# Eight strided transfers in place of one for the first weight load of a decode kernel

## The chip, the cores and the metric

The kernel runs on one core of a Trainium2 chip. The metric is the device time of one execution in microseconds; a version's time is the median of its runs.

## The reference

One decode step, with 8 sequences (B), one token each, model width D = 576. Two branches read the same token and a gate mixes them.

```python
x = A_x                                             # [8, 1, 576]
g = sigmoid((x * gate_w).sum(-1, keepdims=True))
# A: attention over a cache, 32 heads of 128, 4096 cached positions
q = (x @ wq).reshape(8, 1, 32, 128).transpose(0, 2, 1, 3)
scores = einsum("bhqd,bhkd->bhqk", q, k_cache) * 128 ** -0.5
o = einsum("bhqk,bhkd->bhqd", softmax(scores), v_cache)
a = o.transpose(0, 2, 1, 3).reshape(8, 1, 4096) @ wo
# B: layer norm, 576 -> 4608, gelu, 4608 -> 576
h = gelu(layernorm(x) @ w1 + b1)
b = h @ w2 + b2
return g * a + (1 - g) * b
```

All tensors are bfloat16. The two caches hold 8 x 32 x 4096 x 128 elements each, 537 MB together; wq and wo are 4.7 MB each, w1 and w2 5.3 MB each.

## The kernel before

**Tiles.** The caches are read in 32 groups (NG), one for 8 heads (HB) of one sequence. A group's K is one tile of 128 partitions x 256 positions x 128 elements, 64 KB for each partition, and its V likewise. K goes to the buffer `KR`, V to the buffer `VB`. Each group is: product of K with the broadcast q on DVE (L499), sums of it on PE (L510 and L189), a last sum on DVE (L522), softmax, then V times the weights on PE (L563).

**Queues.** Big loads are all issued by SP, in the order in which they are written in the program; `load` (L295) issues one transfer with a semaphore of its own, `load_k` (L327) and `load_v` (L338) those of a later group. SP holds back an issue until the buffer that it fills has been read. ACT's queue carries four small loads at the start: x, the gate row, b1, b2. The order at the start of SP's queue is wq (into `VB`, which V does not need yet), two halves of the first K tile, w1 (into the upper part of `KR`), then w2, which waits for the q projection as it overwrites wq's place, then the second K tile, which waits until the first has been multiplied, then the first V.

**wq.** wq is read flat: its 576 x 4096 elements are cut into 128 runs of `WQR` = 18432 elements (36 KB), one for each partition, so a partition holds four and a half rows of wq. That is one transfer with 128 contiguous runs. The list `ld_wq` holds what has to be waited for.

**The q projection.** x is transposed into nine pieces with a mask for odd and even partitions (`transposed`, L424 to L430), and the layer norm's y after it in the same way. Then 36 matmuls of 128x512 (L183 and L189) multiply the pieces of x with wq as it lies. The first of them waits for `ld_wq`. Its result is scaled (L452), spread over the partitions (L464, L468), and one group's q is copied to `q_n` (L474), which the first product with K needs. The issue of w2, and of the first part of V, waits for the last of these matmuls (`p_Q`).

**After the loop.** The last V comes in four parts and wo in five, so that work can begin on each as it lands; two halves of the result go out on SP and ACT.

Of the kernel before, what the change touches and what calls it, by code (L numbers as in the profile page):

```python
# [41 lines left out]
class Stream:  # L42
# [11 lines left out]
    def op(self, engine, fn, waits=(), dma=None, side=0):  # L54

        rec = [fn, [w for w in waits if w is not None], None, dma, (engine, side)]
        self.ops[engine].append(rec)
        if dma is not None:
            return ("dma", *dma)
        return ("op", engine, rec)  # L60
# [84 lines left out]
def bass_gated_mix__mha_block_cached__mixer_channel_mlp__decode_kernel(  # L145
# [18 lines left out]
    op = S.op  # L164
# [7 lines left out]
    def view(t, offset, shape):  # L172
        ap = []
        stride = 1
        for n in reversed(shape[1:]):
            ap.insert(0, [stride, n])
            stride *= n
        return bass.AP(tensor=t, offset=offset, ap=[[pstride(t), shape[0]]] + ap)
# [22 lines left out]
    WQR = D * SK // 128  # L201
    NXH = 2 * D // 128
    wq_sb = view(VB, 0, [128, WQR])
# [90 lines left out]
    def load(engine, dst, src, name, waits=()):  # L294
        return op(engine, lambda e: e.dma_start(dst, src), waits, dma=(nc.alloc_semaphore(name), 16))  # L295
# [6 lines left out]
        return bass.AP(tensor=t.tensor, offset=t.offset, ap=[[0, B], [1, D]])  # L302


    ld_wq = [load("sync", wq_sb, bass.AP(tensor=A_wq.tensor, offset=A_wq.offset, ap=[[WQR, 128], [1, WQR]]), "ld_wq")]


    def kv_src(cache, n):
# [603 lines left out]
```

## Time and profile before

| | |
|---|---|
| median of 3 runs | 1295.15 us (1295.01 to 1296.24) |
| profiled execution | 1295.46 us, span 1293.5 us |
| PE, DVE, ACT busy | 733.1, 854.5, 72.9 us |
| bytes moved by DMA | 557.07 MB, 431 GB/s over the span |
| SP's queue | 99.7% of the time of 16 DMA engines |
| wq, from issue to landing | 13.8 us |

The span runs from the first instruction to the last of the profiled execution; the execution's own time has 2.0 us more around it. A share of DMA is the mean busy share of the core's 16 DMA engines. In short stretches of the span this share and the GB/s are rough, since a transfer's packets are long. The lines of the timeline give an instruction's start and duration in microseconds, engine, line, operation, output and inputs, and in brackets the engine's idle time before it and what ended it. DMA instructions on SPq and ACTq are the issues; the data follow later.

### The profile page before, as it was taken

The page shows a single profiled execution, that of the slowest core. Times are in us where ns is not written, and L with a number is a line of the kernel's source. Part 1 is how long each engine was busy: PE and PEld are TensorE (multiplying, and loading weights), DVE is VectorE, ACT ScalarE, POOL GpSimd, SP SyncE. Part 2 cuts the span into 40 slices and gives each one's busy share as a digit, 9 for nine tenths or more (in the row PEclk, how much of TensorE's full clock was granted, in tenths as well). Part 3 has the DMA queues.
Part 4 walks back from the last instruction along what each step waited for, and adds up shares of the span by engine and source line. Part 5 has one row for each costly group of instructions (what it writes and reads, how often), then busy time and mean ns, then how long its engine had stood idle before and what let it go on. Part 6 is the DMA issues. An engine that isn't in the chain of part 4 may idle for free.

```text
span 1293.5 us, 10984 instructions
## 1 busy us (share of the span) xinstructions
PE 733.1 (57%) x4893; PEld 139.4 (11%) x3047; DVE 854.5 (66%) x1081; ACT 72.9 (6%) x162; POOL 12.3 (1%) x21
## 2 busy tenths in 40 slices
PE   3755556455556555556555556555556555556556
PEld 0211111011111011111011111001111001111003
DVE  4646667766667766667766667766668766667763
ACT  3200000000000000000000000000000000000001
POOL 0100000000000000000000000000000000000001
PEclk8877898787899777888778888877898787799778
DMA  9999999999999999999999999999999999999998
GB/s 405 430 445 424 436 436 428 440 432 428 446 426 434 438 428 436 436 428 444 426 432 442 428 434 438 426 440 432 428 446 426 434 438 428 434 438 428 444 432 344
DMA packets 11440, 557.07 MB, mean 431 GB/s; under 512 B 1416, under 2 KB 1576, under 8 KB 1832
## 3 DMA queue, kind: packets, MB, share of 16 engines
q1 hardware_dynamic: 11232, 556.93, 99.7%
q8 instruction: 5, 0.08, 0.0%
q10 hardware_dynamic: 200, 0.03, 0.0%
q14 instruction: 3, 0.02, 0.0%
HBM read 556.95 MB, written 0.01 MB: 431 GB/s over the span
## 4 chain that ended last, share of the span: by engine, by line
DMA 67%; DVE 18%; PE 9%; issue 5%; DVEq 1%; SPq 0%
DMA KR<-in_A_k_cache_dram 65%; DVE p L499 15%; PE psb L189 8%; DVE s_sb L522 2%; DMA KR<-in_A_wo_dram 2%; PE psb L510 2%; DVEq L522 0%; DVEq L137 0%; SPq L295 0%; PE psb L767 0%; PE psb L464 0%; DVE p L863 0%; DVEq L499 0%
## 5 line engine op out<-in xcount | busy, mean ns | idle before, releaser
L499 DVE TENSOR_TENSOR p<-KR,q_n 128x4096 bf16<-128x4096 bf16 x256 | 581.5, 2282 | 208.3 <-DMA KR<-in_A_k_cache_dram 208.3
L189 PE MATMUL psb<-p,ident 128*128 128x512 bf16 x1792 | 489.0, 419 | 0.0
L510 PE MATMUL psb<-p,ident 128*128 128x512 bf16 x256 | 112.5, 439 | 508.9 <-DVE p L499 508.9
L522 DVE TENSOR_REDUCE s_sb<-psb 128x512 f32 (+1 forms) x256 | 175.1, 684 | 108.6 <-PE psb L189 62.0
L510 PEld LDWEIGHTS psb<-p,ident 128*128 128x128 bf16 x256 | 26.3, 103 | 965.9 <-DVE p L499 965.3
L563 PE MATMUL psb<-VB,P 128*32 128x512 bf16 x1984 | 112.7, 380 | 0.0
L551 DVE TENSOR_SCALAR P<-E,own 128x256 bf16<-128x256 bf16 x256 | 53.5, 282 | 87.4 <-ACT E L548 87.4
L474 ACT ACTIVATE q_n<-q_bc 128x128 bf16<-128x128 bf16 x32 | 9.9, 310 | 873.9 <-DVE p L499 873.8
L563 PEld LDWEIGHTS psb<-VB,P 128*32 128x32 bf16 x1984 | 50.0, 97 | 48.1
L580 PE MATMUL psb<-selO,O_sb 128*128 128x8 f32 x256 | 33.9, 259 | 22.5 <-ACT O_sb L575 22.5
L580 PEld LDWEIGHTS psb<-selO,O_sb 128*128 128x128 f32 x256 | 31.0, 191 | 38.3 <-ACT O_sb L575 38.3
L575 ACT ACTIVATE O_sb<-psb 128x512 f32<-128x512 f32 x32 | 19.1, 597 | 197.5 <-PE psb L563 197.5
L570 PEld LDWEIGHTS psb<-rs,ones 128*128 128x128 f32 x64 | 12.1, 190 | 46.6 <-issue 44.4
L695 POOL TENSOR_TENSOR p<-OT_sb,fine 128x512 bf16<-128x512 bf16 (+1 forms) x4 | 5.0, 1275 | 1199.3 <-PE psb L570 1195.5
L548 ACT ACTIVATE E<-s_sb,mD 128x256 bf16<-128x256 f32 x32 | 16.0, 499 | 0.0
L539 DVE TENSOR_REDUCE mA<-s_sb 128x1 f32<-128x256 f32 x32 | 13.4, 420 | 1.1
L479 ACT ACTIVATE OT_sb<-O_n,G 128x8 bf16<-128x8 f32 x31 | 9.3, 301 | 84.3 <-DVE O_n L586 84.3
L554 DVE TENSOR_REDUCE es<-E 128x1 f32<-128x256 bf16 x32 | 13.1, 410 | 0.0
L570 PE MATMUL psb<-rs,ones 128*128 128x8 f32 x64 | 9.2, 216 | 1.3 <-DVE O_n L586 1.3
L428 PE MATMUL psb<-ident,p 8*128 8x8 bf16 x18 | 0.8, 164 | 15.2 <-ACT p L425 13.5
L555 DVE TENSOR_SCALAR rs<-own,es 128x8 f32<-128x8 f32 x32 | 7.5, 234 | 1.1
L657 PE MATMUL psb<-VB,hT_sb 128*8 128x288 bf16 x72 | 6.4, 354 | 2.6 <-POOL hT_sb L636 2.6
(103 smaller groups left out, 129.6 us busy)
## 6 DMA issues: line engine op xcount, KB each, us to landing
KR<-in_A_k_cache_dram SPq DMA_DIRECT2D x2, 4096.0 KB, 27.8
VB<-in_A_v_cache_dram SPq DMA_DIRECT2D x1, 5376.0 KB, 29.5
KR<-in_B_w_dram SPq DMA_DIRECT2D x1, 5184.0 KB, 45.4
VB<-in_B_w_dram SPq DMA_DIRECT2D x1, 5184.0 KB, 40.3
VB<-in_A_wq_dram SPq DMA_DIRECT2D x1, 4608.0 KB, 13.8
KR<-in_A_v_cache_dram SPq DMA_DIRECT2D x1, 4096.0 KB, 22.3
VB<-in_A_v_cache_dram SPq DMA_DIRECT2D x1, 2816.0 KB, 38.1
KR<-in_A_wo_dram SPq DMA_DIRECT2D x1, 2304.0 KB, 20.7
```

Source lines behind the costliest of these rows:

```text
L189: return e.add_instruction(mybir.InstMatmult(name=nc.get_next_instruction_name(), engine=mybir.EngineType.PE, ins=[e.lower_ap(rhs), e.lowe ...
L499: v_mult[n, c] = op("vector", lambda e: e.tensor_tensor(out=p1[:, par, :, :], in0=k_of(), in1=qb, op=ALU.mult), [k_land[n, s], a_q[n], p_s ...
L510: fn = lambda e, r=r: e.matmul(tr_ps[par][:, :], lhsT=ident[:, :], rhs=r, start=True, stop=False)
L522: v_red[n, c] = op("vector", lambda e: e.tensor_reduce(out=s_of(), in_=tr_ps[par][:, :].rearrange("p (t c) -> p t c", c=CH), axis=AX.X, op ...
L539: t = op("vector", lambda e: e.tensor_reduce(out=mA[:, 0:1], in_=s_sb[:, :], axis=AX.X, op=ALU.max), [v_red[n, NC - 1], c_mA])
L548: a_exp[n] = op("scalar", lambda e: e.activation(out=E[:, :], in_=s_sb[:, :], func=ACT.Exp, bias=mD[:, 0:1], scale=1.0), [v_nm[n], v_P.get ...
L551: v_P[n] = op("vector", lambda e, h=h: e.tensor_scalar(out=P[:, :, h, :], in0=E[:, :].rearrange("p (q t) -> p q t", t=TQ), scalar1=own[:, ...
L554: t = op("vector", lambda e: e.tensor_reduce(out=es[:, :], in_=E[:, :], axis=AX.X, op=ALU.add), [a_exp[n]])
L563: p_pv[n] = op("tensor", lambda e, o=o, tq=tq, at=at, v=v: e.matmul(o, lhsT=P[:, tq, :, :].rearrange("p h t -> p (h t)"), rhs=v.rearrange( ...
L570: p_z[n] = op("tensor", lambda e: e.matmul(oz_ps[:, HB:2 * HB], lhsT=ones[:, :], rhs=rs[:, :], start=True, stop=True), [v_rs[n], v_norm.ge ...
L575: a_ev[n] = op("scalar", lambda e: e.activation(out=O_sb[:].rearrange("p t d -> p (t d)"), in_=o_ps[n // last][:, :], func=ACT.Copy), [p_p ...
L580: p_oz[n] = op("tensor", lambda e, tt=tt: e.matmul(o, lhsT=O_sb[:, tt, :], rhs=selO[:, tt, :], start=(tt == 0), stop=(tt == TQ - 1 and stop)),
```

## The change

wq's load is written as eight transfers instead of one. Transfer i takes the runs i, i + 8, i + 16 and so on, sixteen runs, and writes them to the partitions with the same numbers. So every partition gets the same bytes as before. All eight raise one semaphore, each by 16, and what waits for wq waits for the last count, 128. All eight are issued by SP, one after another, ahead of K.

```diff
-    ld_wq = [load("sync", wq_sb, bass.AP(tensor=A_wq.tensor, offset=A_wq.offset, ap=[[WQR, 128], [1, WQR]]), "ld_wq")]
+    s_wq = nc.alloc_semaphore("ld_wq")
+    for i in range(8):
+        w = bass.AP(tensor=A_wq.tensor, offset=A_wq.offset + i * WQR, ap=[[8 * WQR, 16], [1, WQR]])
+        ld_wq = [op("sync", lambda e, i=i, w=w: e.dma_start(wq_sb[i:128:8, :], w), dma=(s_wq, 16 * (i + 1)))]
```

## The prediction

> **What bounds the kernel now.** I read the page from the top: the shares, the 40 slices, the queues, then the chain that ended last.
>
> ```profile
> span 1293.5 us, 10984 instructions
> ...
> DMA  9999999999999999999999999999999999999998
> GB/s 405 430 445 424 436 436 428 440 432 428 446 426 434 438 428 436 436 428 444 426 432 442 428 434 438 426 440 432 428 446 426 434 438 428 434 438 428 444 432 344
> ...
> q1 hardware_dynamic: 11232, 556.93, 99.7%
> ...
> DMA 67%; DVE 18%; PE 9%; issue 5%; DVEq 1%; SPq 0%
> DMA KR<-in_A_k_cache_dram 65%; DVE p L499 15%; PE psb L189 8%; DVE s_sb L522 2%; DMA KR<-in_A_wo_dram 2%; PE psb L510 2%; DVEq L522 0%; DVEq L137 0%; SPq L295 0%; PE psb L767 0%; PE psb L464 0%; DVE p L863 0%; DVEq L499 0%
> ```
>
> The sixteen DMA engines are busy in every slice, and SP's queue, q1, which carries wq, K, V and the weights, fills 99.7% of their time. Only the first slice (405) and the last (344) fall below the rest. The chain names DVE and PE too, but it walks only the waits of K. To see whether their time is extra I cut the span into stretches: width, busy time (and instructions) of PE, PEld, DVE, ACT, POOL, then the granted clock, the DMA share, GB/s.
>
> ```profile
> 0.00:2.00 2.00, 0.00 (x0) 0.00 (x0) 0.49 (x3) 1.25 (x1) 1.15 (x9) 1.00 0.70 184
> 2.00:4.00 2.00, 0.00 (x0) 0.00 (x0) 1.00 (x3) 1.12 (x3) 0.00 (x0) 1.00 0.54 184
> 4.00:14.50 10.50, 0.38 (x9) 0.32 (x9) 3.99 (x13) 5.47 (x10) 0.30 (x1) 1.00 1.01 431
> 14.50:24.50 10.00, 4.34 (x49) 1.57 (x49) 1.39 (x4) 2.21 (x4) 0.00 (x0) 0.89 1.00 430
> ...
> 100.00:1260.00 1160.00, 657.52 (x4138) 113.45 (x2460) 789.90 (x991) 49.44 (x121) 0.00 (x0) 0.84 1.00 433
> 1260.00:1280.00 20.00, 15.36 (x182) 7.37 (x166) 11.20 (x24) 2.59 (x5) 5.72 (x5) 0.91 0.97 413
> ```
>
> From 4 us on, the engines move 430 to 433 GB/s at a share of 1.00, whatever they read: 433/16 = 27 GB/s for each. That is a cap, and the kernel lives on it. So a microsecond that the DMA engines lose anywhere before 1260 us is lost at the end, unless the queue runs dry somewhere later and has slack to give. It does not: here are SP's issues (start, duration) and the times to landing.
>
> ```profile
> 0.74 0.41 SPq L295 DMA_DIRECT2D VB<-in_A_wq_dram  x1
> 1.21 0.89 SPq L295 DMA_DIRECT2D KR<-in_A_k_cache_dram  x2
> 2.14 0.60 SPq L295 DMA_DIRECT2D KR<-in_B_w_dram  x1
> 19.57 0.33 SPq L295 DMA_DIRECT2D VB<-in_B_w_dram  x1
> 47.77 0.33 SPq L327 DMA_DIRECT2D KR<-in_A_k_cache_dram  x1
> ...
> 91.92 0.33 SPq L327 DMA_DIRECT2D KR<-in_A_k_cache_dram  x1
> 108.78 0.33 SPq L338 DMA_DIRECT2D VB<-in_A_v_cache_dram  x1
> ```
>
> ```profile
> KR<-in_B_w_dram SPq DMA_DIRECT2D x1, 5184.0 KB, 45.4
> VB<-in_B_w_dram SPq DMA_DIRECT2D x1, 5184.0 KB, 40.3
> VB<-in_A_wq_dram SPq DMA_DIRECT2D x1, 4608.0 KB, 13.8
> ```
>
> wq lands at 0.74 + 13.8 = 14.5 us, w1 at 2.14 + 45.4 = 47.5, w2 at 19.57 + 40.3 = 59.9. The second K tile is issued at 47.77, 12.1 us before w2 has drained, so the queue always has its next transfer. From here each K and V follows in the same way.
>
> **The change, part by part.**
>
> *Seven more issues on SP.* The duration of one is in the rows of the helper's line (minimum, median, maximum ns):
>
> ```profile
> L295 SPq DMA_DIRECT2D KR<-in_A_wo_dram x5: 383/433/433, 1225.6 to 1267.1; - x5
> L295 SPq DMA_DIRECT2D KR<-in_A_v_cache_dram x4: 327/374/433, 1253.1 to 1265.2; - x4
> ```
>
> Eight at 0.33 to 0.43 us, 0.05 us between them, take 3.0 to 3.9 us in place of 0.41. The two K halves and w1 stand behind them on SP: K's first issue moves from 1.21 to about 3.8 to 4.6 us, w1's from 2.14 to about 5. K's data are not wanted by the engines before wq has drained near 14.5 us. So this costs 0; were that cover gone, it would cost 2.6 to 3.4 us. w2's issue waits for the q projection, 19.57 us, and does not move for this reason. ACT's queue (x, the gate row, b1, b2) is not passed by anything.
>
> *Feeding the engines.* One new transfer is 576 KB, 0.59 MB; at 433 GB/s it lasts 1.36 us, against an issue of 0.4. The queue stays ahead: 0.
>
> *Joints between transfers.* What seven more joints cost is seen best near the end, where SP issues V's four parts and wo's four:
>
> ```profile
> 1253.12 12.48 SPq L295 DMA_DIRECT2D KR<-in_A_v_cache_dram  x4
> 1265.65 1.85 SPq L295 DMA_DIRECT2D KR<-in_A_wo_dram  x4
> 1291.61 0.37 SPq L868 DMA_DIRECT2D out_dram<-p  x1
> ```
>
> There eight transfers go through in line at 413 instead of 433 GB/s in 20 us: 20 x 20/433 = 0.92 us for eight, 0.8 for seven. The other bound is 0, by wq, K and w1, which join at 431 and 430. I take 0, since wq's runs stay long (36 KB each), like those. [...]
>
> *The first bytes.* The first two stretches move 184 GB/s each: 2 x 2 x (433-184)/433 = 2.3 us are lost, 1.15 us of them by 1.15 us, when the only wq issue ends. If sixteen runs are described sooner than 128, the gain is at most the other 1.15 us. At the other end it is 0. I take -0.2: the engines must in any case fetch their first run, and nothing shows that 0.41 us of issue would shrink.
>
> *The wait.* The q projection waits for one semaphore at 128 instead of one at 16. It is the same wait, on PE, once: 0. Behind it on PE stand only the broadcast of q and the first key sums, which need q.
>
> *Which partitions are written together.* This is the only term with a size. Before, a transfer spans 128 partitions; after, it spans 16 that lie eight apart, and four transfers in a row have offsets 0 to 3 before offsets 4 to 7 come. No row shows a large transfer over a part of the partitions. The cap of 27 GB/s is the same for K, V, wq and the weights, with runs of different lengths, so it is not the source's: it sits either in the sixteen engines or on sixteen paths into the memory that they write. If in the engines, this term is 0. If on the paths, it matters which partitions are hit together: where paths own blocks of four neighbours, every eighth partition reaches every second block alone, two engines stand on one path, and the other half of the paths idle until the fifth transfer. wq's 4.72 MB then take twice 4.72/0.433 = 10.9 us, so this end is +10.9 us. Engines that are ahead enter the other half early; by no more than about an issue (0 to 0.4 us), I take -0.2.
>
> [...]
>
> I take the upper end. Every row at the cap has one thing in common, 128 partitions in one transfer, and this change takes away just that; no row shows an engine above 27 GB/s or the cap holding without it.
>
> Sum: 0 + 0 + 0 - 0.2 + 0 + 10.9 - 0.2 = +10.5 us. The profiled execution took 1295.46 us (span 1293.5 and 2.0 around it), 0.3 above the median of 1295.15; I set the sum on the median: 1305.6.
>
> **What hides nothing, and what is late next.** If wq lands at 25 us, everything in the queue behind it shifts alike. The other inputs of the q projection:
>
> ```profile
> 1.72 0.57 ACTq L295 DMA_DIRECT2D p<-in_A_x_dram  x1
> ...
> 8.98 0.74 DVE L403 TENSOR_REDUCE stat<-p 8x1 f32<-8x576 bf16 x1 [5.98 <-DMA p<-in_A_x_dram]
> ...
> 15.92 3.60 PE L189 MATMUL psb<-VB,p 128*16 128x512 bf16 x36
> ...
> 21.30 0.31 ACT L474 ACTIVATE q_n<-q_bc 128x128 bf16<-128x128 bf16 x1
> 24.42 2.29 DVE L499 TENSOR_TENSOR p<-KR,q_n 128x4096 bf16<-128x4096 bf16 x1 [8.09 <-DMA KR<-in_A_k_cache_dram]
> ```
>
> x (7.3 us after its issue) waits its turn between wq's runs. The layer norm of it stands ahead of the q projection on PE, which starts 1.4 us after wq landed. With runs at half speed x may come some 7 us later, still before wq; the projection then starts right after wq, and q_n is ready about 6 us later, 4 us before the first K half, which also comes 10.5 later. So DVE's first product moves with K, to about 35 us, and the second K issue to about 58, with w2 still draining. Nothing downstream absorbs the shift, and nothing adds to it.
>
> **Rivals.**
>
> *The cap sits in the engines (not slower), 0.30.* Each engine has the same eight runs of wq as before. Terms: 0 for the paths, 0 to +0.8 for joints, -1.15 to 0 for first bytes: 1294.0 to 1296.0, most likely 1295.0. For it: the same 27 GB/s in every row, as a limit of an engine would show. Against it: nothing; the rows cannot part it from the forecast. It decides if 4:14.5 us still shows about 430 GB/s.
>
> *Faster from an early start, 0.01.* All that is lost at the front is 2.3 us; even the whole of it is under the 0.2% (2.6 us) that a measurement of this kernel tells from no change.
>
> *Transfers of one queue stand in line, 0.03.* The last output transfer starts at 1291.61 and the span ends 1.9 us later, with 4.5 KB to move: that is about a bare transfer. Seven of them are 13 us: 1308. Against it stand 430 GB/s across the joints of wq and K.
>
> *A partial sharing, 0.05.* A path may carry more than one engine brings, but not two: between 0 and +10.5, say +5: 1300.
>
> **How the numbers follow.** Forecast 0.60, engines 0.30, partial 0.05, in line 0.03, early start 0.01, unnamed 0.01. Slower by over 0.2% are forecast, partial and in line: 0.68; same: engines, 0.31 with the unnamed; faster 0.01. The time is the forecast's, 1305.6; its own range is 1304 (a first-byte gain of 1.15 and drift of 0.4) to 1307 (joints at +0.8 and no gain). As the engines' case holds 0.30, the range must reach it: 1294.2 to 1308.
>
> **What the changed profile would show.** For the forecast: eight wq issues of 576 KB, ending near 4 us; GB/s about 216 from 4 us to 25 us while the DMA share stays near 1.0, because each run lasts twice as long; the first K product at 35 us instead of 24.42; the second K issue near 58 us; from there on the old rhythm of K and V and the same 433 GB/s. If the first ten microseconds still show 430 GB/s, the paths are not shared and the prediction is wrong by its one large term. If the share itself falls below 1.0 in that stretch, the engines wait between transfers, and the joints were mis-sized.

## The result and the profile after

The changed kernel takes 1307.05 us (median of 22 runs; 1306.64 to 1307.52), the kernel before 1295.05: a ratio of 1.0085, interval 1.0071 to 1.01, or 12.0 us more. The profiled execution took 1307.13 us, with a span of 1305.3, 11.8 us over the 1293.5 of before.

The page of the changed kernel, its slices and the queue of the large loads:

```profile
span 1305.3 us, 10991 instructions
...
DMA  9999999999999999999999999999999999999998
GB/s 242 438 432 443 426 438 428 438 428 438 430 438 430 436 432 432 436 428 440 426 442 426 442 426 442 424 444 424 444 424 444 424 442 426 442 426 440 428 430 359
...
q1 hardware_dynamic: 11344, 556.93, 99.6%
```

The bytes are the same, and so is the busy share of the DMA engines, in every slice. Only the first slice tells: 242 GB/s in place of 405. Busy at a lower rate means that the engines are not short of work; each piece of it lasts longer (2.87 us for a run of wq in place of 1.36, below). The same by stretches, the columns as before:

```profile
0.00:2.00 2.00, 0.00 (x0) 0.00 (x0) 0.49 (x3) 1.26 (x1) 1.15 (x9) 1.00 0.00 0
2.00:4.00 2.00, 0.00 (x0) 0.00 (x0) 0.99 (x3) 0.65 (x3) 0.00 (x0) 1.00 1.31 295
4.00:14.50 10.50, 0.00 (x0) 0.00 (x0) 3.41 (x10) 5.91 (x10) 0.30 (x1) 1.00 1.10 227
14.50:24.50 10.00, 0.77 (x18) 0.72 (x22) 1.90 (x5) 0.73 (x2) 0.00 (x0) 1.00 0.87 178
24.50:34.50 10.00, 4.19 (x40) 1.21 (x36) 0.00 (x0) 1.50 (x3) 0.00 (x0) 0.96 1.03 416
...
110.00:1270.00 1160.00, 655.61 (x4138) 113.58 (x2459) 790.26 (x989) 49.45 (x121) 0.00 (x0) 0.84 1.00 433
```

From 4 to 24.5 us it is 227 and 178 GB/s where 431 and 430 stood; over both, (227 x 10.5 + 178 x 10)/20.5 = 203. From 110 us on it is 433, as before. SP's issues and the instructions that wait for wq, from the timeline:

```profile
0.74 5.04 SPq L308 DMA_DIRECT2D VB<-in_A_wq_dram  x8
5.83 1.05 SPq L295 DMA_DIRECT2D KR<-in_A_k_cache_dram  x2
6.93 0.43 SPq L295 DMA_DIRECT2D KR<-in_B_w_dram  x1
30.66 0.33 SPq L295 DMA_DIRECT2D VB<-in_B_w_dram  x1
59.33 0.33 SPq L330 DMA_DIRECT2D KR<-in_A_k_cache_dram  x1
...
103.74 0.33 SPq L330 DMA_DIRECT2D KR<-in_A_k_cache_dram  x1
```

```profile
9.86 0.74 DVE L406 TENSOR_REDUCE stat<-p 8x1 f32<-8x576 bf16 x1 [6.87 <-DMA p<-in_A_x_dram]
...
26.84 3.78 PE L189 MATMUL psb<-VB,p 128*16 128x512 bf16 x36 [9.70 <-DMA VB<-in_A_wq_dram]
...
36.23 4.50 DVE L502 TENSOR_TENSOR p<-KR,q_n 128x4096 bf16<-128x4096 bf16 x2 [18.74 <-DMA KR<-in_A_k_cache_dram]
```

Before, the q projection on PE began at 15.92 us with wq already there; now PE waits 9.70 us for wq. K's first product moves from 24.42 to 36.23 (+11.8), K's second issue from 47.77 to 59.33 (+11.6), the third K issue from 91.92 to 103.74 (+11.8), the end by 11.8. The shift is made in the first 27 us and then carried to the end unchanged.

The trace also holds each packet. One packet is one run of wq on one engine; in order of their starts, sixteen at a time, their mean durations in us are:

```
run            1st   2nd   3rd   4th   5th   6th   7th   8th    sum   then K's first run
before         2.15  1.36  1.36  1.36  1.36  1.37  1.37  1.37  11.70  1.22
changed        2.62  2.87  2.85  2.86  2.74  2.86  2.86  2.87  22.53  1.81
```

### The profile page after: what moved, and what is told of

It reads as the page before. It is cut to its first block, busy times and chain, and to the rows that moved or that the text cites. A ratio compares the mean times of both kernels' runs of the same rounds, so it can differ in the third digit from the quotient of the medians.

```text
span 1305.3 us, 10991 instructions
## 1 busy us (share of the span) xinstructions
PE 730.6 (56%) x4893; PEld 139.5 (11%) x3047; DVE 854.9 (65%) x1081; ACT 72.9 (6%) x162; POOL 12.4 (1%) x21
## 4 chain that ended last, share of the span: by engine, by line
DMA 67%; DVE 17%; PE 9%; issue 5%; DVEq 1%; SPq 0%
DMA KR<-in_A_k_cache_dram 65%; DVE p L502 15%; PE psb L189 7%; DVE s_sb L525 2%; DMA KR<-in_A_wo_dram 2%; PE psb L513 2%; DVEq L525 0%; DVEq L137 0%; SPq L308 0%; SPq L295 0%; PE psb L770 0%; PE psb L467 0%; DVE p L866 0%; DVEq L502 0%
## 5 line engine op out<-in xcount | busy, mean ns | idle before, releaser
L557 DVE TENSOR_REDUCE es<-E 128x1 f32<-128x256 bf16 x32 | 13.2, 413 | 0.0
L189 PE MATMUL psb<-VB,p 128*16 128x512 bf16 x36 | 3.8, 601 | 9.7 <-DMA VB<-in_A_wq_dram 9.7
```

The lines of the kernel that those rows point to most:

```text
L189: return e.add_instruction(mybir.InstMatmult(name=nc.get_next_instruction_name(), engine=mybir.EngineType.PE, ins=[e.lower_ap(rhs), e.lowe ...
L557: t = op("vector", lambda e: e.tensor_reduce(out=es[:, :], in_=E[:, :], axis=AX.X, op=ALU.add), [a_exp[n]])
```

## The experiments

Theory P is the one behind the forecast: sixteen paths into the memory that is written, each for blocks of four partitions, and a transfer that reaches half of them moves at half the rate. It is a supposition of the author: no trace of before shows a path, and no run below counts them; what the runs show is the rate for each set of partitions. The rivals are N, each transfer or issue has a price (12 us for seven more), and S, the source addresses that are read side by side matter. They are tried on the wq load alone; `W8` is `WQR // 8`.

**Eight transfers that each reach all partitions.**

```diff
-        w = bass.AP(tensor=A_wq.tensor, offset=A_wq.offset + i * WQR, ap=[[8 * WQR, 16], [1, WQR]])
-        ... wq_sb[i:128:8, :]
+        w = bass.AP(tensor=A_wq.tensor, offset=A_wq.offset + i * W8, ap=[[WQR, 128], [1, W8]])
+        ... wq_sb[:, i * W8:(i + 1) * W8]
```

> wq again in eight transfers on one semaphore, but cut along the run: each takes an eighth (4.5 KB) of all 128 partitions. Theory P (paths into the written memory, each for blocks of four partitions): all sixteen paths are reached by every transfer, so the loss goes away: 1295 to 1297 us, 4 to 14.5 us at about 425 GB/s. Rival N (the number of transfers or of issues costs): eight transfers as in the changed kernel, about 1307 us. Rival S (the source addresses that are read together): the same addresses are read side by side as in one transfer, 1295 us.

Measured: 1295.63 us against 1294.97, ratio 1.0005 (0.9995 to 1.0014). The interval holds 1, so no difference can be told, though all ten runs (1295.32 to 1295.82) lie above all thirteen of the kernel before (1294.82 to 1295.17). Its timeline and stretches:

```profile
0.75 4.21 SPq L309 DMA_DIRECT2D VB<-in_A_wq_dram  x8
5.00 1.01 SPq L295 DMA_DIRECT2D KR<-in_A_k_cache_dram  x2
```

```profile
4.00:14.50 10.50, 0.78 (x18) 0.73 (x22) 5.21 (x15) 6.18 (x11) 0.30 (x1) 1.00 1.10 444
14.50:24.50 10.00, 4.64 (x40) 1.26 (x36) 0.00 (x0) 1.50 (x3) 0.00 (x0) 1.00 0.98 423
```

The same number of transfers of the same size, nearly as long on SP (4.21 against 5.04 us), K's issue nearly as late: and 444 GB/s instead of 227. N falls: neither the splitting nor the issues on SP cost the 12 us. What is left is which rows a transfer spans, and this run changed the read and the written ones alike; the next three part them.

**Written and read pattern, crossed.** Three kernels with eight transfers of sixteen runs. In the first, both sides are sixteen neighbours; in the second and third, one side keeps the distance of eight.

```diff
 # neighbours to neighbours
+        w = bass.AP(..., offset=A_wq.offset + 16 * i * WQR, ap=[[WQR, 16], [1, WQR]])
+        ... wq_sb[16 * i:16 * (i + 1), :]
 # neighbours read, every eighth partition written
+        w = bass.AP(..., offset=A_wq.offset + 16 * i * WQR, ap=[[WQR, 16], [1, WQR]])
+        ... wq_sb[i:128:8, :]
 # every eighth run read, neighbours written
+        w = bass.AP(..., offset=A_wq.offset + i * WQR, ap=[[8 * WQR, 16], [1, WQR]])
+        ... wq_sb[16 * i:16 * (i + 1), :]
```

> Eight transfers of sixteen neighbouring partitions each (0 to 15, 16 to 31, ...), source runs neighbouring too. Theory P: sixteen neighbours reach four paths of sixteen, four engines share one, a run of 36 KB lasts four times 1.36 = 5.5 us or a little more, wq 44 us in place of 11: +33 to +36 us, 1328 to 1331. Rival N: eight transfers, 1307 us. Rival S: the source is one contiguous piece for each transfer, not strided any more: about 1295 us.

> Each of the eight transfers writes every eighth partition as the changed kernel does, but reads sixteen neighbouring runs (so wq's runs land in other partitions than they belong to). Theory P: only the written partitions count: as the changed kernel, 1306 to 1308 us. Rival S (sources 8 x 36 KB apart read together are slow): gone, 1295 us. Rival N: 1307 us.

> The other half of the cross: sources eight runs apart, as in the changed kernel, written to sixteen neighbouring partitions (runs land in other partitions than they belong to). Theory P: four paths, 1328 to 1331 us. Rival S: as the changed kernel, 1307 us. Rival N: 1307 us.

| read / written | time, us | ratio to before |
|---|---|---|
| neighbours / neighbours | 1324.35 | 1.0226 (1.0209 to 1.0243) |
| neighbours / every eighth | 1306.36 | 1.0088 (1.0071 to 1.0105) |
| every eighth / neighbours | 1324.03 | 1.0224 (1.0207 to 1.0241) |
| every eighth / every eighth (the change) | 1307.05 | 1.0085 (1.0071 to 1.01) |

The times go by the written side; the read side moves them by 0.7 us at most. S falls. The stretches of the kernel with neighbours on both sides:

```profile
4.00:14.50 10.50, 0.00 (x0) 0.00 (x0) 0.00 (x0) 3.09 (x6) 0.00 (x0) 1.00 0.98 113
14.50:24.50 10.00, 0.00 (x0) 0.00 (x0) 2.69 (x10) 1.49 (x2) 0.00 (x0) 1.00 1.05 119
24.50:34.50 10.00, 0.77 (x18) 0.72 (x22) 2.61 (x6) 1.52 (x3) 0.30 (x1) 1.00 1.05 118
```

Sixteen neighbours move 113 to 119 GB/s, near a quarter of 433, again with a full DMA share. P's size was off here: from the second on, the runs last 5.05 to 5.14 us, 3.7 times 1.365 and not 4 or more, so the loss is 29.4 us and not 33 to 36.

**Two transfers, by halves and by every second partition.** Both have 64 partitions for a transfer.

```diff
 # halves
+    for i in range(2):
+        w = bass.AP(..., offset=A_wq.offset + 64 * i * WQR, ap=[[WQR, 64], [1, WQR]])
+        ... wq_sb[64 * i:64 * (i + 1), :]
 # every second
+        w = bass.AP(..., offset=A_wq.offset + i * WQR, ap=[[2 * WQR, 64], [1, WQR]])
+        ... wq_sb[i:128:2, :]
```

> wq in two transfers: partitions 0 to 63, then 64 to 127. Theory P with the map of four-partition blocks in which 64 neighbours reach eight of the sixteen paths: half the rate as long as wq lasts, though only one more transfer than before: 1306 to 1308 us, about 210 GB/s from 4 to 24 us. If 64 neighbours reached all sixteen paths: 1295 us. Rival N (a price for each transfer, 12 us for seven more): 1296.7 us.

> wq in two transfers of 64 partitions again, every second one, so each transfer reaches all sixteen paths. What theory P leaves open is which engine takes which row when an engine has four of them. If the rows are spread over the engines as in the one transfer of 128, so that at any moment all paths are written: 1295 to 1296 us. If an engine takes four rows next to each other in the transfer (partitions 0, 2, 4, 6 for the first engine), all engines stand in every second block at the same time: 1307 us. Rival N: 1296.7 us.

Halves: 1306.83 us, ratio 1.0091 (1.0074 to 1.0107). Every second: 1295.29, ratio 1.0002 (0.9992 to 1.0011). The 4 to 14.5 us row of each, halves first:

```profile
4.00:14.50 10.50, 0.00 (x0) 0.00 (x0) 0.00 (x0) 3.33 (x6) 0.00 (x0) 1.00 1.10 227
```

```profile
4.00:14.50 10.50, 0.38 (x9) 0.32 (x9) 3.79 (x13) 5.76 (x10) 0.30 (x1) 1.00 1.04 446
```

That 64 neighbours reach eight paths was supposed, with the other value beside it; the 227 GB/s decide for half the rate. One more transfer is enough for the whole loss when it covers the wrong partitions, and costs nothing when it covers the right ones.

**Every fourth partition, four transfers.**

```diff
+    for i in range(4):
+        w = bass.AP(..., offset=A_wq.offset + i * WQR, ap=[[4 * WQR, 32], [1, WQR]])
+        ... wq_sb[i:128:4, :]
```

> wq in four transfers of 32 partitions, every fourth one: all sixteen paths are reached, two rows for an engine. Theory P: 1295 to 1296 us if the two rows of an engine are dealt so that all paths are written at any moment; 1307 us if an engine's rows are neighbours in the transfer (0 and 4, 8 and 12, ...) or if rows 0 to 15 go first. Rival N: 1300 us.

1295.46 us, ratio 1.0004 (0.9994 to 1.0013). So a distance of 4 costs nothing and one of 8 takes half the rate (446 against 227 GB/s from 4 to 14.5 us), which fits blocks of four. And if P holds, an engine's two rows are dealt so that all paths are written at once, which the expectation had left open. In these runs 64 or 32 partitions in a transfer, spread, go at the full rate (446 GB/s from 4 to 14.5 us in both).

**Another order of the eight.**

```diff
-    for i in range(8):
+    for n, i in enumerate((0, 4, 1, 5, 2, 6, 3, 7)):
+        ... dma=(s_wq, 16 * (n + 1)))]
```

> The changed kernel's eight transfers in the order 0, 4, 1, 5, 2, 6, 3, 7, so that neighbours in the queue use different halves of the paths. If all engines stay in step, two share a path in each transfer as before: 1306 to 1307 us. If an engine that is ahead can go to the free half while its partner is still on the other, and stays ahead, the loss shrinks, to about 1296 to 1301 us. Rival N: 1307 us.

1305.94 us, ratio 1.0084 (1.0067 to 1.0101): the loss remains, the engines stay in step: the sixteen runs of a transfer begin within 1.1 us of one another, less than half a run. But it is 1.1 us less than the change. Its packets, and those of the halves:

```
run            1st   2nd   3rd   4th   5th   6th   7th   8th    sum   then K's first run
other order    2.57  2.72  2.71  2.73  2.72  2.73  2.72  2.70  21.60  1.59
halves         2.63  2.88  2.88  2.87  2.72  2.87  2.86  2.87  22.57  1.66
```

By P the other order changes the half of the paths with every run; there a run lasts 2.70 to 2.73 us from the second on, twice 1.36. In the change and in the halves, four runs in a row go to one set of partitions (in the change partitions 0 to 3 of each eight, in the halves 0 to 63), then four to the other; there it lasts 2.85 to 2.88, except for the fifth, the first on the other set, with 2.74 and 2.72. That is the 5% by which the sharing was dearer than two for one.

**Both halves at once, from two queues.**

```diff
+    ld_wq = []
+    for i, e in enumerate(("sync", "scalar")):
+        w = bass.AP(..., offset=A_wq.offset + 64 * i * WQR, ap=[[WQR, 64], [1, WQR]])
+        ld_wq.append(load(e, wq_sb[64 * i:64 * (i + 1), :], w, f"ld_wq{i}"))
```

> wq in two halves at the same time: partitions 0 to 63 issued by SP, 64 to 127 by ACT ahead of its small loads. Theory P: each engine takes runs of both queues in turn; if all engines start with SP's half and stay in step, all sixteen stand on the same eight paths: 1305 to 1307 us. If they fall out of step, some on one half and some on the other, the paths are used better: between 1295 and 1305. x and the gate row come later by ACT's longer issue, which is hidden. Rival N: 1296.7 us.

1305.92 us, ratio 1.0083 (1.0066 to 1.01). In the packets, the engines take a run of each queue in turn from the second run to the seventh, all sixteen in the same order (means 2.67 to 2.69 us for the third to the seventh); so two queues end where the other order did. Its timeline has a second lesson:

```profile
29.03 0.74 DVE L406 TENSOR_REDUCE stat<-p 8x1 f32<-8x576 bf16 x1 [26.04 <-DMA p<-in_A_x_dram]
...
35.97 4.01 PE L189 MATMUL psb<-VB,p 128*16 128x512 bf16 x36
```

```profile
64.81 0.33 SPq L330 DMA_DIRECT2D KR<-in_A_k_cache_dram  x1
...
102.04 0.33 SPq L330 DMA_DIRECT2D KR<-in_A_k_cache_dram  x1
```

x comes only at 29.03, as it stands behind wq's half on ACT (the expectation had foreseen only ACT's longer issue), so the q projection begins at 35.97 us, 9 us later than in the changed kernel, and K's second issue at 64.81, 5.5 later. K's third issue is at 102.04, ahead of the changed kernel's 103.74. Here the late work on an engine is absorbed by the lead of K's issue: 5.5 us late at the second, 1.7 us early at the third. The late bytes are not: the kernel takes 10.9 us more than before.

**The same loss elsewhere.** wq in one transfer again, and w2 in two halves:

```diff
-        st["ld_w2"] = load("sync", w2_sb, B_w2.rearrange("(p j) n -> p j n", j=NJ), "ld_w2", [p_Q])
+        s_w2 = nc.alloc_semaphore("ld_w2")
+        w = B_w2.rearrange("(p j) n -> p j n", j=NJ)
+        for i in range(2):
+            p = slice(64 * i, 64 * (i + 1))
+            st["ld_w2"] = op("sync", lambda e, p=p: e.dma_start(w2_sb[p], w[p]), [p_Q], dma=(s_w2, 16 * (i + 1)))
```

> The kernel before with wq in one transfer again, and w2 (5.31 MB, from about 47 us on) in two transfers, partitions 0 to 63 and 64 to 127. Theory P, with a loss that is never given back wherever it falls: w2 takes 12.3 us more, by the measure of wq's halves (11.7 for 10.9) 13.2: 1307.4 to 1308.5 us. Rival F (only the start of the kernel is on the path, later loads have slack, since K's next issue has a lead of 12 us): under 1300 us.

1310.45 us, ratio 1.0118 (1.0101 to 1.0134). Stretches:

```profile
47.50:60.00 12.50, 8.65 (x147) 4.34 (x85) 5.22 (x19) 4.66 (x9) 1.85 (x4) 0.89 1.02 212
60.00:72.50 12.50, 0.30 (x6) 0.00 (x0) 0.00 (x0) 0.44 (x1) 2.17 (x2) 0.50 1.08 233
```

Rival F falls: a loss at w2, from about 47 us on, is not given back either. The loss, 15.4 us, is 2.2 over the 13.2 expected. Sixteen packets at a time, w2's first runs last 3.63 us and the others 3.07 to 3.28 where 1.54 stood, 13.9 us over the eight. Most of the rest lies behind w2: K's first run on each engine, in flight with w2's last, took 4.00 in place of 2.42 us, +1.6, while w1's last run took 1.70 in place of 1.54. Together that is the 15.7 us between the spans (1309.2 and 1293.5). Why K's first runs were slower beside w2's last was not tried by itself.

## Why the prediction was right, point by point

- *The time.* 12.0 us more, against 10.5 foreseen. 1307.05 lies just above the forecast's own range of 1304 to 1307 (by its terms the low end is 1304.5) and inside the wide one. That the rate goes by the partitions written was right: the cross gave 1306.36 us with every eighth partition written and 1324.03 with neighbours written, each with the other's read side. The two terms of -0.2 and the joints, below, account for the 1.5 us that were missing.
- *The bound.* Right: bytes per microsecond set the time. The 11.8 us of the span were lost by 27 us, and neither K's second issue nor the third gave any back.
- *The paths, +10.9.* The loss is shown by the cross of read and written sides and by every second against halves; the paths are not. No row of before could tell paths from engines, as the prediction says itself: that every row at the cap spans 128 partitions fits the engines as well. That paths own blocks of four, and that there are sixteen, was the author's supposition, chosen at 0.60 to 0.30; no run shows or counts a path. What the runs showed in its place is the rate by the partitions written, from 4 to 14.5 us: 444 GB/s for all, 446 for every second and every fourth, 227 for every eighth and for 64 neighbours, 113 for sixteen neighbours. By packets wq's runs grew from 11.70 to 22.53 us, +10.8. That agreement holds two errors that cancel: the first run was slow in both kernels, so it cost 0.5 and not 1.4; the other seven cost 1.48 each and not 1.36, by the 5% above.
- *Drift of the engines, -0.2, and first bytes, -0.2.* These two terms failed. wq's first packets start at 2.45 us on the mean instead of 2.02, so the first bytes cost +0.4. The count of runs to describe does not explain it: sixteen neighbours start at 1.94, 64 neighbours at 2.40. Why is open. And nothing was won at the far end: K's first run, in flight with wq's last, lasted 1.81 instead of 1.22 us, +0.6.
- *Joints.* Taken as 0, at most 0.8. In the changed kernel the gaps between an engine's runs add up to 0.2 us more than before. With these, 10.8 + 0.4 + 0.6 + 0.2 = 12.0: K's second run starts at 27.01 us on the mean instead of 15.01. The medians differ by as much, the spans of the two traces by 11.8. Eight column slices measured 0.7 us more, near that bound, in an interval that holds 1.
- *Issues on SP.* The term was 0 and is 0, but an issue took 0.57 to 0.62 us, not 0.33 to 0.43; K's moved to 5.83, not 4.6. It stayed covered: with the column slices SP takes 4.21 us, and no loss can be told.
- *x.* Foreseen some 7 us late, it came 0.9 us late (9.86 against 8.98): its rows wait for a run or two of wq, not for half of the load. They start between 7.49 and 8.37 us, as wq's third runs do (7.60 to 8.51), and before between 5.32 and 7.17. Nothing hung on it.
- *What the profile should show.* 216 GB/s from 4 to 25 us: 203. First product at 35: 36.23. Second K issue near 58: 59.33. A DMA share near 1.0: 1.10 and 0.87, in rough short stretches, 0.99 over both.
- *The rivals.* The cap in the engines is refuted by halves against every second, where each engine has the same number of runs to move. Transfers standing in line are refuted by the column slices. A partial sharing is refuted where P puts two engines on a path: the runs last 2.72 to 2.87 us, twice 1.36 or a little more. Where it puts four, at 5.05 to 5.14 us, 3.7 times, it shows slightly. An early start did not come, wq's first packets were later.

## What to carry to other kernels

Before splitting a load by partitions, ask which partitions are written at the same moment: in these runs every second or every fourth partition was free (446 GB/s), every eighth, or a half, took twice the time (2.87 us a run in place of 1.36), and sixteen neighbours nearly four times (5.05 to 5.14). If a load has to be split, cut it along the row, so that every piece spans all 128 partitions: eight such pieces ran at 444 GB/s, with no difference in time that can be told. A DMA share of 1.0 does not say that bytes move at the full rate (here 227 GB/s stood beside 1.10): read the GB/s beside it, and in a kernel bound by bytes take each microsecond lost there as lost at the end: here it was so with wq at the start (11.8 us of the span) and with w2 some 45 us on (15.7).

## What the runs showed of the hardware

- The loss is not in whole steps. Sixteen engines write 16 x 36.9 KB to sixteen neighbours in 5.1 us, 116 GB/s; to every eighth partition in 2.87 us, 206 GB/s, and in 2.72 us, 217 GB/s, in the other order; with one transfer over all partitions in 1.364 us, 432 GB/s. So the neighbours get over a quarter of the full rate, and every eighth a half or a little less.
- Writing run after run to one set (partitions 0 to 3 of each eight, then 4 to 7; or 0 to 63, then 64 to 127) costs 5% more than changing between 0 to 3 and 4 to 7 of each eight with every run, 2.87 against 2.72 us. Why is open.
- An issue on SP is not of one price: 0.41 us for wq in one transfer (the kernel before), 0.57 for one of its halves (two queues), 0.59 (median) for a sixteen-partition transfer (the change).
- In the run with two queues, the engines that serve them in turn stayed in step with each other through the whole of wq: in each round sixteen runs of about 2.7 us, all of one queue, begin within 1.8 us.
